# Moving transpositions, key maxima and value sums within the first group of a fused attention and feed-forward kernel

## The chip, the cores and the metric

One Trainium2 chip, one core. The metric is the device time of one execution in microseconds (us), as the median over runs. Engines are named as in the profile: PE (TensorE), DVE (VectorE), ACT (ScalarE), POOL (GpSimd), SP (SyncE, which issues all DMAs here).

## The reference, cut to what matters

Local attention with block summaries for 4 batches, 8 heads, 768 positions and head size 64, then a feed-forward block over 3072 tokens:

```
k_sum = k.reshape(B,H,24,32,D).max(axis=3)      # maximum of each block of 32 keys
v_sum = v.reshape(B,H,24,32,D).mean(axis=3)     # mean of each block of 32 values
scores = concat(scale*q@k.T within a window of 16, scale*q@k_sum.T + log(32))
x = softmax(scores) @ concat(v, v_sum)          # -> (3072, 512)
h = x @ w_in                                    # (3072, 2048)
g = h * tanh(softplus(h));  out = g @ w_out     # (3072, 512)
```

The weights come in as float64 and every product of the feed-forward block is made of three float32r products (high by high, low by high, high by low).

## The kernel before, in words

A **unit** is 256 queries (chunk c of 12, three to a batch) and two heads (hp of 4): 48 units. A **group** of the feed-forward part is 512 tokens, two chunks; there are six groups, and each has 16 **steps**, one for each 128 columns of the hidden layer. The program order of each engine is written out by hand, and every engine works in that order.

The lead-in (L480 to L509, turns u = 0 to 10) makes the eight units of group 0: scores on PE (L321, L323), minus their row maximum on DVE (L339), exponentials on ACT (L343), normalising on DVE and POOL (L353 to L357), transposing on PE with a copy on ACT (L365, L367), values on PE (L397), and the result's high part xh on ACT (L399) and low part xl on DVE (L400). Between these it prepares weights.

A weight **piece** is two steps' worth of w_in or w_out, 1 MB in two DMAs (L124); pieces are numbered w0 to w15 in the order of need (w3 is w_in of steps 4 and 5, w7 of 8 and 9, w11 of 12 and 13). Each passes four calls: *begin* (rebase on ACT L140, two shifts on DVE L144 and L146, after which the next piece is loaded into the freed one of two staging buffers), *join* (DVE L154, L156), *upper* (ACT L164) and *lower* (DVE L171).

The loop L524 runs the steps. Step i issues ff_in(i) on PE (12 products, L412), act(i) and, in the first group, the copy ah(i) on ACT (L419, L428), al(i) on DVE (L430), and at its end ff_out(i-2) on PE (12 products, L440). Into the steps the later units are woven in pairs (n, m). Scores of a pair stand in steps 0, 4, 8, 12, 15, 19 and so on; in the first group the pair is normalised one step later, transposed two steps later (L592, after ff_out), and its values (L397) stand in steps 4, 8, 12 and 15. While pair p stands in its steps, the next pair is prepared: key maxima (km, L250, from the keys' source ks) and value sums (vq, L270 and L271, from vsum), needed only where a new batch begins. In the first group those are the pairs whose scores stand in steps 8 and 12. For such a pair: step 4 (8) takes n's maxima and loads n's vsum (L211); step 5 (9) takes n's sums, stores them (L272) and loads m's ks (L207); step 6 (10) takes m's maxima, loads m's vsum, and POOL copies both units' maxima into the score operands (L281); step 7 (11) takes m's sums, stores them, and loads the next ks if there is one. Step 3 loads the first ks. The sources ks and vsum share a single buffer, so this is one chain of load and reduction. PSUM has four buffers in ps_w for products, scores, transposed blocks and values.

In steps 2, 3, 6, 7, 10 and 11, DVE's order is al(i), then m's maxima or sums, then join, begin and lower. On SP the loads L211, L272 and L207 stand ahead of the piece's load L124 of the same step.

Of the kernel before, what the change touches and what calls it, by code (L numbers as in the profile page):

```python
# [28 lines left out]
CPB = S // CH  # L29
# [3 lines left out]
NFC = DFF // P  # L33
# [19 lines left out]
def _as_f32(bits):  # L53
    import struct
    return struct.unpack("<f", struct.pack("<I", bits))[0]
# [3 lines left out]
def fused_kernel(ctx: ExitStack, tc: tile.TileContext, q0, qk, kt, v0, vw, vs, w_in, w_out, out):  # L59
# [46 lines left out]
    def home(j, part, dtype, name):  # L106

        if j == NW:
            t = stage.tile([P, WB, WP], I64, tag="stage", name=name).bitcast(dtype)
            return t.rearrange("p k f -> p (k f)")[:, :WB * WP]  # L110
        pool = const if j < EARLY else late[0]
        return pool.tile([P, WB * WP], dtype, tag=f"w{part}_{j}", name=name, bufs=1)
# [37 lines left out]
    def join_weight():  # L150
        if begun:
            w, fc, f, x = begun.pop(0)
            u = f.bitcast(U32)
            nc.vector.tensor_scalar(out=f, in0=f, scalar1=-_as_f32(F32_MAX), scalar2=_as_f32(F32_MAX),  # L154
                                    op0=ALU.max, op1=ALU.min)
            nc.vector.scalar_tensor_tensor(out=u, in0=u, scalar=3, in1=x,  # L156
                                           op0=ALU.logical_shift_left, op1=ALU.bitwise_or)
            joined.append((w, fc, f))

    def upper_weight():  # L160
        if joined:
            w, fc, f = joined.pop(0)
            split[w, fc, 0] = home(order[w, fc], 0, F32R, f"w{w}_{fc}_hi")
            nc.scalar.copy(split[w, fc, 0], f)  # L164
            raised.append((w, fc, f))

    def lower_weight():
        if raised:
            w, fc, f = raised.pop(0)
            split[w, fc, 1] = home(order[w, fc], 1, F32R, f"w{w}_{fc}_lo")  # L170
            nc.vector.tensor_sub(split[w, fc, 1], f, split[w, fc, 0].bitcast(F32))  # L171
# [9 lines left out]
    for part, step, at0 in ((blocks[:, :NQ], QT, -WIN), (blocks[:, NQ:], P, CH)):  # L181
        n = part.shape[1]
# [22 lines left out]
    def load_key_source(b, hp):  # L205
        ks = sources[b, hp, 0] = stage.tile([P, S], F32, tag="sum", name=f"ks{b}_{hp}", bufs=1)
        nc.sync.dma_start(ks, kt[b, hp])  # L207

    def load_value_source(b, hp):
        vsum = sources[b, hp, 1] = stage.tile([VP, BLK, BLK], F32, tag="sum", name=f"vsum{b}_{hp}", bufs=1)  # L210
        nc.sync.dma_start(vsum, vs[b, hp].rearrange("p (d j) -> p d j", j=BLK))  # L211
# [11 lines left out]
    def first_key_summary(hp):  # L223
        key_summary(0, hp, keys0[hp][:, WIN:])
# [22 lines left out]
    def key_summary(b, hp, keys):  # L247

        km = att.tile([P, NB], F32, tag="km", name=f"km{b}_{hp}", bufs=HP)
        nc.vector.reduce_max(km, keys.rearrange("p (n j) -> p n j", j=BLK), axis=AX.X)  # L250
        summary[b, hp] = [km]
# [27 lines left out]
    def att_block_keys(c, hp):  # L279
        km = summary[c // CPB, hp][0]  # L280
        nc.gpsimd.tensor_copy(units[c, hp]["qk"][:, :, P + KW:], km.unsqueeze(1).broadcast_to([P, NQ, NB]))  # L281

    def att_summarize_keys(c, hp):
        b, th = divmod(c, CPB)
        if th == 0:
            key_summary(b, hp, sources.pop((b, hp, 0)))
            load_value_source(b, hp)

    def att_summarize_values(c, hp):
        b, th = divmod(c, CPB)  # L290
        if th == 0:
            value_summary(b, hp)
# [66 lines left out]
    def att_transpose(group):  # L359
        pt = att.tile([P, 2 * NQ, P], F32, tag="pt", name=f"pt{group[0][0]}_{group[0][1]}", bufs=1)[:KA]  # L360
        for k, (c, hp) in enumerate(group):
            u = units[c, hp]
            ps = att_psum(c, f"pt_ps{c}_{hp}")
            for s in range(NQ):
                nc.tensor.transpose(ps[:KA, s * P:(s + 1) * P], u["p"][:, s, :], ident)  # L365
            u["pt"] = pt[:, k * NQ:(k + 1) * NQ]
            nc.scalar.copy(u["pt"].rearrange("p s q -> p (s q)"), ps[:KA, :])  # L367
# [54 lines left out]
    def ff_split(g, fc):  # L422

        a = st[g, fc]
        ah = ff.tile([P, TG], F32R, tag="ah", name=f"ah{g}_{fc}")
        al = ff.tile([P, TG], F32R, tag="al", name=f"al{g}_{fc}")

        (nc.scalar.copy if g == 0 else nc.vector.tensor_copy)(ah, a)  # L428
        st[g, fc] = ah, al
        return lambda: nc.vector.tensor_sub(al, a, ah.bitcast(F32))  # L430
# [21 lines left out]
    todo = [(c, hp) for c in range(NCH) for hp in range(HP)]  # L452
    steps = [(g, fc) for g in range(NG) for fc in range(NFC)]

    at = {}
# [7 lines left out]
    n = CG * HP  # L463
# [16 lines left out]
    for u in range(n + 3):  # L480
        if u < n:
            att_scores([todo[u]])
        if 1 <= u <= n:
            att_normalize([todo[u - 1]])
        if 1 <= u <= HP:
            first_value_summary(u - 1)
        lower = att_values([todo[u - 3]]) if 3 <= u else None
        if u in (3, 4):
            window_values(*todo[HP + u - 1])
        if HP < u <= n:  # L490
            block_values(*todo[u - 1])
        if 2 <= u < n + 2:
            att_transpose([todo[u - 2]])
        if u in (0, 2):
            first_key_summary(u + 1)
        if lower:
            lower()
        if u in (3, 9):
            lower_weight()
        if u in (2, 8, 10):  # L500
            join_weight()
            upper_weight()
        if u in (1, 6, 8, 10):
            begin_weight()
            load_weight()
        if u == 1:
            first_key_summary(u + 1)
        if u in (7, 8):
            att_load_values(*todo[u + 1])  # L509
# [5 lines left out]

    turns = sorted(at)
    values = dict(zip(turns[1:] + [turns[-1] + 4], (at[i] for i in turns)))
    turned = {i + 2: group for i, group in at.items() if i < NFC - 1}
    following = dict(zip(turns, (at[i] for i in turns[1:])))
    lower_weight()  # L520
    join_weight()
# [2 lines left out]
    for i in range(len(steps) + 2):  # L524
        if i - 1 in at and i < NFC:
            att_normalize(at[i - 1])
        if i < len(steps):
            ff_in(*steps[i])
            ff_act(*steps[i])
            if i < NFC:  # L530
                split_rest = ff_split(*steps[i])
        if i - 1 in at:
            upper_weight()
            rebase_weight()
        if i < NFC and i - 1 in following:

            att_summarize_values(*following[i - 1][0])
        group = values.get(i)
        lower = att_values(group) if group else None
        if lower and i >= NFC:  # L540
            lower()
        if i in at:
            att_scores(at[i], i >= NFC - 1)
        if i < NFC:
            if lower:
                lower()
            split_rest()
        if i - 1 in at and i >= NFC:
            att_normalize(at[i - 1])
        if i - 3 in at and i - 3 >= NFC - 1:  # L550
            att_transpose_blocks(at[i - 3], 1)
        if NFC <= i < len(steps):
            ff_split(*steps[i])()
        if i - 2 in at and i - 2 >= NFC - 1:
            att_transpose_blocks(at[i - 2], 0)
        if i - 3 in following:
            n, m = following[i - 3]
            att_summarize_values(*m)
            after = todo.index(m) + 1
            if after < len(todo) and todo[after][0] % CPB == 0:  # L560
                load_key_source(todo[after][0] // CPB, todo[after][1])
        if i in following:
            n, m = following[i]
            att_summarize_keys(*n)
            for unit in (n, m):
                att_load_keys(*unit)
        if i - 1 in following:
            n, m = following[i - 1]
            if i >= NFC:
                att_summarize_values(*n)  # L570
            if m[0] % CPB == 0:
                load_key_source(m[0] // CPB, m[1])
        if i - 2 in following:
            n, m = following[i - 2]
            att_summarize_keys(*m)
            for unit in (n, m):
                att_block_keys(*unit)
        if i not in at:
            upper_weight()
        join_weight()  # L580
        begin_weight(i in at)
        load_weight()
        if i not in at:
            lower_weight()
        if i - 1 in at:
            lower_weight()
        if group:
            for unit in at.get(i, ()):
                att_load_values(*unit)
        if i >= 2:  # L590
            ff_out(*steps[i - 2])
        if i in turned:  # L592
            att_transpose(turned[i])


# [42 lines left out]
```

## Time and profile before

| | us |
|---|---|
| median of 3 runs (633.32 to 637.02) | 635.2 |
| the profiled execution's own time | 637.01 |
| its span | 635.1 |
| PE busy in it | 606.7 |
| DVE busy | 384.4 |
| ACT busy | 258.9 |

The span is the stretch from the first to the last instruction; times in rows count from its start. Busy is the union of an engine's instructions. In a row of the timeline, the bracket at the end gives how long the engine sat idle just before and which instruction's end released it.

### The profile page before, as it was taken

What the parts mean: (1) busy time and instruction counts of PE and PEld (TensorE: products, weight loads), DVE (VectorE), ACT (ScalarE), POOL (GpSimd) and SP (SyncE); (2) the same over time, 40 slices, a digit from 0 to 9 for tenths busy, and PEclk for the clock granted to TensorE, in tenths of its full rate; (3) what the DMA queues carried; (4) which work ended last, traced back from release to release, by engine and by line L of the source; (5) the groups of instructions that cost most, each with busy time, mean ns of one, the idle gap of its engine ahead of it and who ended that gap; (6) DMA issues with size and microseconds to landing.
All of it is one profiled execution on the core that took longest, in us unless ns stands there. A gap on an engine that the chain in (4) does not pass through costs nothing.

```text
span 635.1 us, 10801 instructions
## 1 busy us (share of the span) xinstructions
PE 606.7 (96%) x4096; PEld 496.5 (78%) x4096; DVE 384.4 (61%) x1032; ACT 258.9 (41%) x630; POOL 75.9 (12%) x119
## 2 busy tenths in 40 slices
PE   4858998899999999999999999999999999999997
PEld 3746876778888888788888888888888888888886
DVE  4678998884656668756637659757547546222211
ACT  3768875768144144253153253253352241111111
POOL 3441010102011010120110110110110110000000
PEclk9979999999999999999999999999999999999999
DMA  8946686733123042632032242532231110100001
GB/s 274 325 148 244 224 271 206 262 123 97 67 96 102 20 146 63 206 117 92 4 96 88 82 144 72 171 98 69 87 103 59 38 33 0 67 0 1 0 1 66
DMA packets 31779, 69.26 MB, mean 109 GB/s; under 512 B 4720, under 2 KB 11120, under 8 KB 31728
## 3 DMA queue, kind: packets, MB, share of 16 engines
q1 hardware_dynamic: 31728, 68.58, 33.8%
q8 instruction: 32, 0.52, 0.3%
q14 instruction: 19, 0.16, 0.1%
HBM read 60.16 MB, written 6.29 MB: 105 GB/s over the span
## 4 chain that ended last, share of the span: by engine, by line
PE 78%; DVE 8%; ACT 5%; DMA 4%; issue 3%; SPq 1%; POOL 0%; DVEq 0%; ACTq 0%; POOLq 0%
PE po L440 36%; PE ph L412 34%; PE x_ps L397 3%; PE sc L317 2%; DMA ks<-kt 2%; ACT pr L343 2%; DVE w_lo L171 2%; DMA vw<-vw 1%; DVE x L144 1%; DVE f L154 1%; ACT f L140 1%; DVE x L146 1%; DMA w<-w_out 1%; DVE km L250 1%; DVE al L430 1%
## 5 line engine op out<-in xcount | busy, mean ns | idle before, releaser
L419 ACT ACTIVATE a<-ph 128x512 f32<-128x512 f32 x96 | 57.4, 598 | 283.7 <-PE ph L412 230.2
L412 PE MATMUL ph<-xh,w_hi 128*128 128x512 f32 x384 | 151.2, 394 | 2.5 <-DVE nm L339 2.3
L440 PE MATMUL po<-w_hi,ah 128*128 128x512 f32 x384 | 152.0, 396 | 0.2 <-DVE o L448 0.2
L412 PE MATMUL ph<-xl,w_hi 128*128 128x512 f32 x384 | 150.3, 391 | 0.0
L412 PE MATMUL ph<-xh,w_lo 128*128 128x512 f32 x384 | 150.2, 391 | 0.0
L440 PE MATMUL po<-w_lo,ah 128*128 128x512 f32 x384 | 149.7, 390 | 0.0
L440 PE MATMUL po<-w_hi,al 128*128 128x512 f32 x384 | 149.6, 390 | 0.0
L428 DVE CAST ah<-a 128x512 fp32r<-128x512 f32 x80 | 34.8, 435 | 143.9 <-ACT a L419 143.4
L378 DVE STREAM_TRANSPOSE pt<-pr 32x256 f32<-32x256 f32 x256 | 111.6, 436 | 3.6
L412 PEld LDWEIGHTS ph<-xh,w_hi 128*128 128x128 f32 x384 | 72.6, 189 | 18.8 <-issue 2.1
L440 PEld LDWEIGHTS po<-w_hi,ah 128*128 128x128 f32 x384 | 72.1, 188 | 18.0 <-issue 3.0
L412 PEld LDWEIGHTS ph<-xh,w_lo 128*128 128x128 f32 x384 | 72.5, 189 | 15.3
L412 PEld LDWEIGHTS ph<-xl,w_hi 128*128 128x128 f32 x384 | 72.6, 189 | 14.8
L440 PEld LDWEIGHTS po<-w_lo,ah 128*128 128x128 f32 x384 | 72.1, 188 | 15.3
L440 PEld LDWEIGHTS po<-w_hi,al 128*128 128x128 f32 x384 | 72.2, 188 | 14.3
L343 ACT ACTIVATE pr<-pr,nm 128x120 f32<-128x120 f32 x192 | 73.2, 382 | 19.3 <-DVE nm L339 19.0
L357 POOL TENSOR_TENSOR pr<-pr,rs 128x960 f32<-128x960 f32 (+1 forms) x28 | 44.3, 1581 | 225.3 <-DVE rs L354 147.2
L430 DVE TENSOR_TENSOR al<-a,ah 128x512 fp32r<-128x512 f32 x96 | 66.6, 694 | 6.5 <-ACT ah L428 3.8
L397 PEld LDWEIGHTS x_ps<-pt,vw 120*64 120x64 f32 x768 | 26.0, 143 | 16.7 <-issue 8.6
L400 DVE TENSOR_TENSOR xl<-x_ps,xh 128x512 fp32r<-128x512 f32 (+1 forms) x28 | 17.2, 613 | 34.9 <-ACT xh L399 34.5
L397 PE MATMUL x_ps<-pt,vw 120*64 120x64 f32 x768 | 29.8, 231 | 8.2 <-POOL pr L357 3.7
L343 ACT ACTIVATION_READ_ACCUMULATOR pr<-pr,nm 128x1 f32 x192 | 35.8, 187 | 0.0
(59 smaller groups left out, 455.8 us busy)
## 6 DMA issues: line engine op xcount, KB each, us to landing
qk<-qk SPq DMA_DIRECT2D x40, 496.0 KB, 4.2
vw<-vw SPq DMA_DIRECT2D x48, 192.0 KB, 5.2
w<-w_in SPq DMA_DIRECT2D x16, 512.0 KB, 4.6
w<-w_out SPq DMA_DIRECT2D x16, 512.0 KB, 4.6
ks<-kt SPq DMA_DIRECT2D x16, 384.0 KB, 4.4
out<-o SPq DMA_DIRECT2D x24, 256.0 KB, 2.3
vsum<-vs SPq DMA_DIRECT2D x12, 384.0 KB, 3.3
vw<-vm SPq DMA_DIRECT2D x40, 48.0 KB
```

What stands on the lines that cost most here:

```text
L171: nc.vector.tensor_sub(split[w, fc, 1], f, split[w, fc, 0].bitcast(F32))
L317: nc.tensor.matmul(ps[h][row, at0:at0 + KA], u["qk"][r, s, h * QT:(h + 1) * QT], u["qk"][r, s, P:], start=True, stop=True)
L343: nc.scalar.activation(pr[:, j, :], pr[:, j, :], AF.Exp, scale=-1.0, bias=nm[:, j:j + 1], accum_out=sm[:, j:j + 1])
L357: nc.gpsimd.tensor_mul(u["pr"], u["pr"], rs.unsqueeze(2).broadcast_to([P, n, KA]))
L378: nc.vector.transpose(u["tr"][b * SQ:(b + 1) * SQ, :, a * SQ:(a + 1) * SQ], u["wide"][a * SQ:(a + 1) * SQ, :, b * SQ:(b + 1) * SQ])
L397: nc.tensor.matmul(x, u["v"][:, s, d], pt, start=True, stop=True)
L400: return lambda: nc.vector.tensor_sub(xl, x, xh.bitcast(F32))
L412: nc.tensor.matmul(ph, w[:, cc * P:(cc + 1) * P], x[:, cc, :], start=(cc == 0 and n == 0), stop=(cc == NCC - 1 and n == 2))
L419: nc.scalar.activation(a, st[g, fc], AF.Mish)
L428: (nc.scalar.copy if g == 0 else nc.vector.tensor_copy)(ah, a)
L430: return lambda: nc.vector.tensor_sub(al, a, ah.bitcast(F32))
L440: nc.tensor.matmul(po[g][t], a[:, tok], w, start=(fc == 0 and n == 0), stop=(fc == NFC - 1 and n == 2))
```

## The change

In the lead-in, w1 begins in turn 7 and not 6, its *upper* comes in turn 9 and not 8 (so after w2's *begin*), and its *lower* in turn 10 and not 9. In the first group the transposition of a pair moves from the end of the second step after its scores (behind ff_out) into the third (behind ff_in, act and ah). The calls for m's maxima and the copies (step 2, 6, 10, 14) and for m's sums with the next ks (step 3, 7, 11, 15) move, in the first group alone, from ahead of the step's weight work to behind it. From step 16 on, the order is what it was.

```
-        if u in (3, 9):
+        if u in (3, 10):
             lower_weight()
         if u in (2, 8, 10):
             join_weight()
+        if u in (2, 9, 10):
             upper_weight()
-        if u in (1, 6, 8, 10):
+        if u in (1, 7, 8, 10):
             begin_weight()
             load_weight()
...
-    turned = {i + 2: group for i, group in at.items() if i < NFC - 1}
+    turned = {i + 3: group for i, group in at.items() if i < NFC - 1}
...
             if i < NFC:
                 split_rest = ff_split(*steps[i])
+            if i in turned:
+                att_transpose(turned[i])
...
-        if i - 3 in following:
-            n, m = following[i - 3]
-            att_summarize_values(*m)
-            ...
-                load_key_source(todo[after][0] // CPB, todo[after][1])
+        def last_sum():
+            if i - 3 in following:
+                ... the same five lines
+        def last_maxima():
+            if i - 2 in following:
+                n, m = following[i - 2]
+                att_summarize_keys(*m)
+                for unit in (n, m):
+                    att_block_keys(*unit)
+        if i >= NFC:
+            last_sum()
...
-        if i - 2 in following:
-            ...
+        if i >= NFC:
+            last_maxima()
         if i not in at:
             upper_weight()
         join_weight()
         begin_weight(i in at)
         load_weight()
         ...
             lower_weight()
+        if i < NFC:
+            last_maxima()
+            last_sum()
         ...
             ff_out(*steps[i - 2])
-        if i in turned:
-            att_transpose(turned[i])
```

## Rows read from the trace of the kernel before

**Rows 1.** The page's line of busy time by engine.

```profile
PE 606.7 (96%) x4096; PEld 496.5 (78%) x4096; DVE 384.4 (61%) x1032; ACT 258.9 (41%) x630; POOL 75.9 (12%) x119
```

**Rows 2.** Busy time by stretch: the stretch, its length, then the busy us of each engine (instructions), PE's granted clock, DMA share, GB/s.

```profile
100.00:125.00 25.00, 20.98 (x106) 16.49 (x107) 24.33 (x47) 16.77 (x32) 3.30 (x3) 1.00 0.75 238
...
150.00:300.00 150.00, 149.80 (x1027) 122.95 (x1024) 98.42 (x292) 58.66 (x155) 17.46 (x24) 1.00 0.33 104
```

**Rows 3.** PE's timeline, the rows with an idle time of note before them, and the values of step 15: start, us, engine, line, operation, operands.

```profile
38.78 0.42 PE L397 MATMUL x_ps<-pt,vw 120*64 120x64 f32 x7 [2.88 <-POOL pr L357]
...
62.54 0.65 PE L365 MATMUL pt_ps<-ident,pr 128*120 128x128 f32 x4 [1.83 <-POOL pr L357]
...
88.82 0.43 PE L365 MATMUL pt_ps<-ident,pr 128*120 128x128 f32 x2 [1.10 <-POOL pr L357]
...
100.20 0.64 PE L317 MATMUL sc<-qk 64*64 64x120 f32 x16 [0.45 <-POOL qk L281]
...
111.27 0.47 PE L412 MATMUL ph<-xh,w_hi 128*128 128x512 f32 x1 [1.53 <-DVE nm L339]
...
119.09 0.65 PE L365 MATMUL pt_ps<-ident,pr 128*120 128x128 f32 x4 [2.12 <-POOL pr L357]
...
140.07 0.47 PE L412 MATMUL ph<-xh,w_hi 128*128 128x512 f32 x1 [0.79 <-DVE nm L339]
...
149.35 1.15 PE L397 MATMUL x_ps<-pt,vw 120*64 120x64 f32 x32
```

**Rows 4.** DVE's timeline in the lead-in: xl of the last four units, each behind an idle time, and the first L339 of step 0.

```profile
38.23 0.42 DVE L400 TENSOR_TENSOR xl<-x_ps,xh 128x256 fp32r<-128x256 f32 x1 [1.04 <-ACT xh L399]
...
39.91 0.42 DVE L400 TENSOR_TENSOR xl<-x_ps,xh 128x256 fp32r<-128x256 f32 x1 [0.65 <-ACT xh L399]
...
44.92 0.42 DVE L400 TENSOR_TENSOR xl<-x_ps,xh 128x256 fp32r<-128x256 f32 x1 [0.95 <-ACT xh L399]
...
47.04 0.42 DVE L400 TENSOR_TENSOR xl<-x_ps,xh 128x256 fp32r<-128x256 f32 x1 [0.56 <-ACT xh L399]
...
54.78 0.28 DVE L339 CUSTOM_DVE_ANT_0 pr<-sc,base 128x120 f32<-128x120 f32 x1
```

**Rows 5.** DVE's timeline in steps 4 to 10: the first L339 of step 4 and of step 8, the four key maxima L250, the low parts al ahead of two of them, and the *lower* that ends step 6's weight work.

```profile
79.56 0.27 DVE L339 CUSTOM_DVE_ANT_0 pr<-sc,base 128x120 f32<-128x120 f32 x1
...
82.38 0.94 DVE L250 TENSOR_REDUCE km<-ks 128x24 f32<-128x768 f32 x1
...
94.92 0.68 DVE L430 TENSOR_TENSOR al<-a,ah 128x512 fp32r<-128x512 f32 x1
98.47 0.95 DVE L250 TENSOR_REDUCE km<-ks 128x24 f32<-128x768 f32 x1 [2.87 <-DMA ks<-kt]
...
102.49 1.21 DVE L171 TENSOR_TENSOR w_lo<-f,w_hi 128x1024 fp32r<-128x1024 f32 x1
...
109.84 0.27 DVE L339 CUSTOM_DVE_ANT_0 pr<-sc,first 128x120 f32<-128x120 f32 x1
...
112.66 0.94 DVE L250 TENSOR_REDUCE km<-ks 128x24 f32<-128x768 f32 x1
...
125.19 0.69 DVE L430 TENSOR_TENSOR al<-a,ah 128x512 fp32r<-128x512 f32 x1
128.52 0.95 DVE L250 TENSOR_REDUCE km<-ks 128x24 f32<-128x768 f32 x1 [2.64 <-DMA ks<-kt]
```

**Rows 6.** SP's timeline: the issue of the first ks, of w10 (step 3), and of the sums' store in step 7.

```profile
74.59 0.42 SPq L207 DMA_DIRECT2D ks<-kt  x1
78.61 0.92 SPq L124 DMA_DIRECT2D w<-w_out  x2
...
105.68 0.80 SPq L272 DMA_DIRECT2D vm<-vq  x1
```

**Rows 7.** DMA issues by kind: count, KB each, median us from issue to landing.

```profile
w<-w_out SPq DMA_DIRECT2D x16, 512.0 KB, 4.6
ks<-kt SPq DMA_DIRECT2D x16, 384.0 KB, 4.4
...
vsum<-vs SPq DMA_DIRECT2D x12, 384.0 KB, 3.3
```

**Rows 8.** The chain that ended last, in order of time: start, us, what.

```profile
123.14 5.36 DMA ks<-kt
...
145.79 0.87 PE pt_ps L365 x8
...
154.43 2.72 PE ph L412 x12
```

**Rows 9.** POOL's timeline: the copy of m's maxima that the scores of step 8 wait for.

```profile
99.64 0.51 POOL L281 COPY qk<-km 128x96 f32<-128x96 f32 x1 [9.52 <-DVE km L250]
```

**Rows 10.** Groups of instructions by line and shape: busy us, mean ns of one, idle before.

```profile
L419 ACT ACTIVATE a<-ph 128x512 f32<-128x512 f32 x96 | 57.4, 598 | 283.7 <-PE ph L412 230.2 <-issue 53.3
...
L428 ACT CAST ah<-a 128x512 fp32r<-128x512 f32 x16 | 10.0, 622 | 0.5
L367 ACT COPY pt<-pt_ps 120x512 f32<-120x512 f32 x16 | 8.9, 586 | 0.4 <-PE pt_ps L365 0.4
```

**Rows 11.** Busy time by stretch, around two idle times of PE; columns as in Rows 2, PE's granted clock third from the end.

```profile
41.00:50.00 9.00, 6.51 (x44) 5.23 (x44) 7.46 (x10) 3.84 (x6) 2.31 (x3) 0.50 0.43 151
118.00:120.00 2.00, 0.91 (x9) 0.91 (x9) 1.97 (x4) 2.00 (x3) 2.00 (x2) 1.00 0.94 269
```

More of the change, by code (lines that the diff above doesn't have):

```diff
@@ L555, in fused_kernel @@
             att_transpose_blocks(at[i - 2], 0)
-        if i - 3 in following:
-            n, m = following[i - 3]
-            att_summarize_values(*m)
-            after = todo.index(m) + 1
-            if after < len(todo) and todo[after][0] % CPB == 0:
-                load_key_source(todo[after][0] // CPB, todo[after][1])
+        def last_sum():
+            if i - 3 in following:
+                n, m = following[i - 3]
+                att_summarize_values(*m)
+                after = todo.index(m) + 1
+                if after < len(todo) and todo[after][0] % CPB == 0:
+                    load_key_source(todo[after][0] // CPB, todo[after][1])
+        def last_maxima():
[6 more added lines that the diff above has]
+            last_sum()
         if i in following:
@@ L572, in fused_kernel @@
                 load_key_source(m[0] // CPB, m[1])
-        if i - 2 in following:
[L574 to L577, printed above, removed]
+        if i >= NFC:
+            last_maxima()
         if i not in at:
```

## The prediction

> **What bounds the kernel now.** I began with the page's busy line: PE is busy for 606.7 of 635.1 us [rows 1], so only some 28 us can be gained on it at all. Busy time by stretch says where: from 150 us on PE has no idle time worth naming (149.80 of 150 up to 300 us), while between 100 and 125 us it is busy for 20.98 of 25 and DVE for 24.33 [rows 2]. So the lead-in and the first group decide, and a change there counts by one thing: how much earlier PE comes to its gapless run, which begins with ff_in(14) at 140.07. PE's timeline shows what it waits for: POOL's normalised scores ahead of three transpositions (1.83, 1.10, 2.12), POOL's copy of m's maxima (0.45), and DVE's L339 of steps 8 and 12, which must free a PSUM tile (1.53, 0.79) [rows 3]. DVE's timeline shows why DVE is late: in steps 6 and 10 it stands idle for 2.87 and 2.64 us until the keys' source has landed, with weight work behind [rows 5].
>
> **The lead-in.** DVE's work from 38 us to the first L339 at 54.78 stays the same; what can go is its four waits for xh, 1.04 + 0.65 + 0.95 + 0.56 = 3.2 us [rows 4]. w1's shifts no longer stand ahead of the seventh unit's L339, and w1's *upper* no longer holds ACT, waiting for the join, ahead of w2's rebase and xh. The first wait remains, since xl still follows xh of its unit and w1's shifts now stand behind it: 1.0. The later ones find xh done while DVE joins and shifts. Gain for DVE: 2.2 us; bounds 0 (waits that only move) and 3.2. In steps 0 and 1 ACT, which waits for the same joins, comes as much earlier, so I carry about 2.3 to step 4: its L339 at 77.3 for 79.56 [rows 5].
>
> **The first ks.** L207 of step 3 now stands on SP behind w10's two DMAs, which are issued once w8's shifts are done: 78.61 - 2.3 = 76.3, plus 0.92 to issue them, so ks goes out at 77.2 for 74.59 [rows 6]. Its landing is bounded by 3.3 us (vsum, the same size) and 5.36 (the slow ks) [rows 7, 8]; I take 4.7, a little over the 4.4 of its kind, because 1 MB stands just ahead. So 81.9, bounds 80.5 and 82.6. DVE is ready 2.82 after L339 (79.56 to 82.38 [rows 5]), at 80.1. **It waits some 1.8 us, and L250 stands at 81.9 for 82.38: of the 2.3 gained, 0.5 is left.** Behind the wait stand join and begin of step 4, the normalising and n's sums. The Trainium skill ("DMA: Bandwidth & Descriptors", Queues, rings and completion order) says that each DMA engine takes the descriptors of a queue in ring order; by that ks lands behind the weights, and if it overtook them, at the 3.3 bound, the sum below would be 1.4 better. No row before shows the two in this order.
>
> **Steps 4 to 8.** The 2.87 us wait in step 6 goes: join, begin and lower stand there now, and ks has landed when they end. L339 of step 8: 109.84 - 0.5 - 2.87 = 106.5, and PE's 1.53 goes. But m's maxima come later in the order. al(6) ends at 95.60 - 0.5 = 95.1; the weight work is 103.70 - 99.42 = 4.3; L250 runs from 99.4 to 100.35 for 98.47 to 99.42 [rows 5]. POOL's copy and PE follow by 0.22 + 0.51 + 0.05 [rows 3, 9]: the second half of step 8's scores starts at 101.1 for 100.20, **0.9 later**. PE stands there for some 2 us in place of 0.45. Between that point and ff_in(10) lie 111.27 - 1.53 - 100.20 = 9.5 us [rows 3]; ff_in(10) starts at 110.6 for 111.27. The PSUM tile is free by 107.9 (before, the wait ended 1.43 after its L339), so it holds nothing up any more. m's vsum goes out at 100.4, behind w13's load on SP, and even at 4.6 lands by 105.0; m's sums stand at 100.35 + al 0.65 + weights 4.3 = 105.3, so they need not wait. m's ks, landed at 98.47 before, would do at 99.4 even if it came no earlier.
>
> **The transpositions.** Each now follows an ff_in (2.72 us [rows 8]). POOL's three waits, 5.05 us together, are covered by it; the cover of the first two is worth nothing by itself, since PE runs into the waits for w_lo, for the copies of pt and for the scores just told. Its price is in step 15, where the transposition and the values of the same pair now stand in one step: PE transposes for 0.87 [rows 8], but ACT first does act, 0.60, ah, 0.62, and the first copy, 0.59 [rows 10]. PE stands 1.81 - 0.87 = **0.95 us**; bounds 0 (something later holds PE anyway) and 1.5 (both copies).
>
> **The third ks** (of step 7). Its load follows m's sums, which are now DVE's last work ahead of L339: sums end at 106.5, the store takes 0.80 [rows 6], L207 goes at 107.4. By then w14 has landed, so I take the 3.3 of vsum: 110.7, bounds 110.7 and 112.8 (5.36). DVE is ready at 106.5 + 2.8 = 109.3 and waits 1.4; L250 at 110.7 for 112.66. From there to the end of al(10) it is 125.88 - 112.66 = 13.2 [rows 5], so 123.9; weight work 4.3, L250 to 129.2, copy and PE 0.8: **the second half of step 12's scores starts at 130.0**. Before, it started when the 128.52 maxima were done, at 129.47 + 0.8 = 130.25 by the same steps. Gain 0.25. PE arrives at about 127 (110.6 + five blocks of 2.72 + 0.87 + values and half of the scores, some 1.7) and stands 3 us.
>
> **The sum.** From there PE is gapless but for 0.79, which goes (L339 of step 12 comes earlier by 2.64 and more), and the 0.95 that comes. -0.25 - 0.79 + 0.95 = -0.1 us. On the profiled execution, 637.0 us of its own time for a span of 635.1: 636.9. It lies 1.8 above the median 635.2; so I forecast **635.1 for the median**. The bounds: ks of step 3 shifts everything by -1.4 to +0.7, that of step 7 by 0 to +2.1, step 15 by -0.95 to +0.55: as a sum rarely all at once, 633.0 to 637.8. A measurement of this kernel tells some 0.5% (3.2 us) from no change.
>
> **Rivals.**
> A, the waits at the transpositions count in full: PE is what is late, not the chain of ks and DVE. For it: they are real waits of PE, 5.05 us. Against: DVE's 24.33 of 25, and L250 behind the weight work. 635.2 - 5.05 = 630.1. Chance 0.13.
> B, PE's clock falls in the new wait of 3 us in step 12. In the lead-in an idle time of 2.88 us [rows 3] came ahead of a stretch of 9 us at clock 0.50, the 1.2 GHz level; after the 2.12 in step 10 the clock stayed at 1.00 [rows 11]. The wait I expect is nearer to the first, which did other, light work around it. It decides where PE's idle time comes to about 2.9. Price: half of PE's busy 6.51 up to half of 9, 3.3 to 4.5 us; with -0.1 and the larger, 639.5, which is slower. Chance 0.14. The Trainium skill ("TensorE: Matmul & The Clock Gate", HAM oscillation) says that TensorE left without work falls to half clock and must earn the full one again; it speaks against a change that gathers short waits into a long one.
> C, DVE gains nothing in the lead-in. ks of step 3 then lands at 84.2, and all behind it comes 2.3 later: 637.4, still no change. Chance 0.15.
> Forecast 0.58.
>
> **How the numbers follow.** Faster by over 0.5% is A, 0.13, with a little of the forecast's lower edge: 0.15. Slower is most of B, 0.12, and the worst landings of both ks, 0.02: 0.14. The rest, 0.71, is within 0.5%. The range holds the forecast, C, the smaller halves of A and B (half of 5.05 is 632.7; 3.3 is 638.4): 631.7 to 638.5.
>
> **What would show it.** Right: PE's row for the scores of step 8 and of step 12 idle for 2 to 3 us behind POOL L281; DVE idle ahead of L250 in steps 4 and 8, not in 6 and 10; no PE wait at L365; 0.9 us idle at L397 in step 15; PE gapless from there within 1 us of the old place (values of step 15 at 149.35 before [rows 3]). Wrong: L250 of steps 4 and 8 without a wait; L281 done ahead of PE; a clock below 1.00 after step 12; or step 0's L339 still near 54.8.

## The result, and the profile after

The changed kernel takes 638.7 us (median of 10 runs, 636.8 to 641.1); the kernel before, measured beside it, 635.9 (10 runs, 633.3 to 639.2). The ratio is 1.0052, 95% interval 1.0034 to 1.0070: **slower by 2.9 us**, where no change was forecast. The profiled execution of the changed kernel took 641.06 us (span 639.3), that of the kernel before 637.01.

Busy time by stretch, columns as in [rows 2]:

```profile
100.00:125.00 25.00, 21.73 (x107) 17.86 (x108) 23.29 (x45) 17.42 (x34) 3.66 (x3) 0.93 0.77 248
150.00:300.00 150.00, 148.85 (x1039) 122.17 (x1037) 95.15 (x274) 57.24 (x147) 17.42 (x25) 1.00 0.30 97
```

Past 150 us PE is as busy as before but for one wait (0.95, below). In every profile of this study the run's own time, less the start of step 15's values, is 487.6 to 487.9 us (637.01 - 149.35 = 487.66 before, 641.06 - 153.20 = 487.86 after). So the place of that one row tells the time of an execution: 149.35 before [rows 3], 153.20 after.

DVE after, answering to [rows 4, 5]:

```profile
36.71 0.42 DVE L400 TENSOR_TENSOR xl<-x_ps,xh 128x256 fp32r<-128x256 f32 x1 [1.04 <-ACT xh L399]
...
52.84 0.27 DVE L339 CUSTOM_DVE_ANT_0 pr<-sc,base 128x120 f32<-128x120 f32 x1
...
63.48 0.69 DVE L154 TENSOR_SCALAR f<-f 128x1024 f32<-128x1024 f32 x1 [1.24 <-ACT f L140]
...
78.84 0.27 DVE L339 CUSTOM_DVE_ANT_0 pr<-sc,base 128x120 f32<-128x120 f32 x1
...
84.14 0.95 DVE L250 TENSOR_REDUCE km<-ks 128x24 f32<-128x768 f32 x1 [2.40 <-DMA ks<-kt]
...
101.55 0.94 DVE L250 TENSOR_REDUCE km<-ks 128x24 f32<-128x768 f32 x1
...
108.70 0.28 DVE L339 CUSTOM_DVE_ANT_0 pr<-sc,first 128x120 f32<-128x120 f32 x1
...
112.83 0.95 DVE L250 TENSOR_REDUCE km<-ks 128x24 f32<-128x768 f32 x1 [1.22 <-DMA ks<-kt]
...
125.37 0.69 DVE L430 TENSOR_TENSOR al<-a,ah 128x512 fp32r<-128x512 f32 x1
125.97 0.69 DVE L154 TENSOR_SCALAR f<-f 128x1024 f32<-128x1024 f32 x1
...
130.25 0.97 DVE L250 TENSOR_REDUCE km<-ks 128x24 f32<-128x768 f32 x1
```

One of the four waits for xh is left, and L339 of step 0 comes 1.94 us earlier, as worked out. The waits ahead of L250 have changed sides: none in steps 6 and 10, 2.40 and 1.22 in steps 4 and 8. In step 10 the weight work (five operations) now stands between al (125.37) and the maxima (130.25).

ACT's row behind DVE's wait at 63.48, and SP's for w10 and the first ks [rows 6]:

```profile
50.76 1.14 ACT L140 ACTIVATE f<-w 128x1024 f32<-128x1024 f32 x1 [1.23 <-DMA w<-w_out]
```

```profile
77.90 0.80 SPq L124 DMA_DIRECT2D w<-w_out  x2
78.74 0.43 SPq L207 DMA_DIRECT2D ks<-kt  x1
```

PE, answering to [rows 3], and POOL's two copies [rows 9]:

```profile
103.27 1.08 PE L317 MATMUL sc<-qk 64*64 64x120 f32 x16 [3.53 <-POOL qk L281]
...
113.52 0.39 PE L412 MATMUL ph<-xh,w_hi 128*128 128x512 f32 x1
...
132.60 0.64 PE L317 MATMUL sc<-qk 64*64 64x120 f32 x16 [2.75 <-POOL qk L281]
...
153.20 1.17 PE L397 MATMUL x_ps<-pt,vw 120*64 120x64 f32 x32 [0.95 <-ACT pt L367]
```

```profile
102.71 0.51 POOL L281 COPY qk<-km 128x96 f32<-128x96 f32 x1 [10.82 <-DVE km L250]
...
131.44 1.11 POOL L281 COPY qk<-km 128x96 f32<-128x96 f32 x1 [10.87 <-DVE km L250]
```

No transposition and no ff_in waits any more, the ff_in at 113.52 included. PE's idle time has been gathered into two waits for m's maxima, and there are new ones for the copies of pt: 0.95 in step 15, and 1.78 ahead of the values of step 4 (72.60). Behind both score waits the granted clock (third from the end) falls to 0.50, the 1.2 GHz level:

```profile
102.00:104.00 2.00, 0.73 (x16) 0.70 (x16) 1.97 (x4) 1.95 (x4) 0.51 (x1) 0.72 0.87 330
104.00:106.00 2.00, 2.00 (x12) 1.43 (x5) 2.00 (x3) 0.50 (x1) 0.00 (x0) 0.50 1.02 336
...
132.00:134.00 2.00, 1.40 (x19) 1.10 (x20) 1.97 (x3) 0.00 (x0) 0.55 (x1) 0.90 0.67 197
134.00:136.00 2.00, 2.00 (x7) 1.52 (x6) 1.97 (x3) 0.00 (x0) 0.00 (x0) 0.50 0.00 0
136.00:138.00 2.00, 2.00 (x8) 1.64 (x7) 2.00 (x18) 1.58 (x9) 0.00 (x0) 0.75 0.04 6
```

Between step 12's second half of scores and step 15's values lie 20.60 us; before there were 19.10, 0.79 of waiting among them.

Two theories were set against each other. **K**: the loss is the late start of m's maxima, behind the weights. **Q**: it is the granted clock behind PE's gathered wait. The rival to both was that the loss lies in another part of the change.

### The profile page after: what moved, and what is told of

Its sections match the earlier page's. It is cut to its first block, busy times and chain, and to the rows that moved or that the text cites. A ratio compares the mean times of both kernels' runs of the same rounds, so it can differ in the third digit from the quotient of the medians.

```text
span 639.3 us, 10797 instructions
## 1 busy us (share of the span) xinstructions
PE 608.0 (95%) x4096; PEld 497.4 (78%) x4096; DVE 384.3 (60%) x1032; ACT 259.2 (41%) x630; POOL 75.5 (12%) x119
## 4 chain that ended last, share of the span: by engine, by line
PE 78%; DVE 8%; DMA 7%; ACT 3%; issue 3%; SPq 0%; POOL 0%; DVEq 0%; POOLq 0%; ACTq 0%
PE po L440 37%; PE ph L412 34%; PE x_ps L397 3%; PE sc L317 3%; DMA ks<-kt 2%; DMA w<-w_out 2%; DMA q<-qk 1%; DVE x L144 1%; DMA vw<-vw 1%; DVE w_lo L171 1%; ACT pr L343 1%; DMA vsum<-vs 1%; DVE x L146 1%; DVE f L154 1%; DVE km L250 1%
## 5 line engine op out<-in xcount | busy, mean ns | idle before, releaser
L339 DVE CUSTOM_DVE_ANT_0 pr<-sc,base 128x120 f32<-128x120 f32 x128 | 31.4, 276 | 8.2 <-PE sc L317 7.6
```

Of the source, the lines that this page charges most:

```text
L339: nc.vector.tensor_tensor_reduce(out=pr[:, j, :], in0=ps[h][:, at0:at0 + KA], in1=m, scale=-SCALE, scalar=-NEG, op0=ALU.add, op1=ALU.min, ...
```

## The experiments: one part of the change alone

Four kernels, each the kernel before with one part of the diff and nothing else, on one chip (before: 635.26 us).

The lead-in's three conditions alone:

```
-        if u in (3, 9):
+        if u in (3, 10):
             lower_weight()
         if u in (2, 8, 10):
             join_weight()
+        if u in (2, 9, 10):
             upper_weight()
-        if u in (1, 6, 8, 10):
+        if u in (1, 7, 8, 10):
             begin_weight()
             load_weight()
```

> The kernel before with the lead-in's edits alone. Theory K (the end of the first group is set by when POOL has copied m's maxima ahead of the scores of steps 8 and 12, and the change puts those copies later): the lead-in alone moves no maxima, so DVE's first L339 comes about 1.9 us earlier (54.78 to 52.9), some 0.7 of it is left at step 4, and the end moves by 0 to -0.7 us. Theory Q (the loss is mostly PE's clock, which falls in waits made longer): PE gets a wait of over 4 us for act(0) ahead of ff_in(2), the clock falls there, and if that reached the end it would cost 1.5 to 2.5 us; I expect it to be hidden behind DVE. Ratio 0.999 to 1.000 by K, up to 1.004 if the clock's fall counts.

634.73 us, ratio 0.9994 [0.9973, 1.0015]. Its profile, of a run at the median (634.65), has L339 of step 4 at 77.31, just where the prediction had it, and DVE's waits in steps 6 and 10 are still 2.67 and 2.25 us.

The transpositions alone:

```
-    turned = {i + 2: group for i, group in at.items() if i < NFC - 1}
+    turned = {i + 3: group for i, group in at.items() if i < NFC - 1}
...
                 split_rest = ff_split(*steps[i])
+            if i in turned:
+                att_transpose(turned[i])
...
             ff_out(*steps[i - 2])
-        if i in turned:
-            att_transpose(turned[i])
```

> The kernel before with the transpositions in the third step alone. K: maxima and sums stay, so the scores of steps 8 and 12 start where they did (100.2 and 130.25); the covered waits for POOL (1.83, 1.10, 2.12 us) only become longer waits at the scores, and step 15 costs 0.95 us for the copies: +0.9 us. Q: PE now stands about 3 us at the scores of steps 8 and 12, the clock falls there and some 1.5 us more is lost after step 12: +2 to +2.5 us. A third view, that the transpositions' waits counted in full: -5 us.

636.11 us, 1.0017 [0.9994, 1.0040]. In its profile the waits at L365 are gone and step 15 has its wait of 0.95; nothing is gained in the median. (The profiled run, 633.97, is 2.1 below it.)

The maxima and copies alone (`last_maxima` holds the lines that stood there):

```
+        if i >= NFC:
+            last_maxima()
         if i not in at:
             upper_weight()
...
         if i - 1 in at:
             lower_weight()
+        if not (i >= NFC):
+            last_maxima()
```

> The kernel before with m's maxima and the copies behind the weight work alone (sums where they were). K: the copies come 1.4 us later (maxima at about 99.9 instead of 98.47), so the second half of the scores of steps 8 and 12 starts about 1.4 us later, and m's sums now wait for vsum on DVE, about 3 us, ahead of the weight work: +0.6 to +1.4 us. Q: the waits at the scores grow to about 2 us only, the clock stays up and the cost is no more than K's. If the late maxima cost nothing, the theory K is wrong.

639.13 us, 1.0063 [1.0040, 1.0086]: slower by itself. With m's sums left where they were, DVE also runs into this:

```profile
106.70 1.22 DVE L270 TENSOR_REDUCE vq<-vsum 96x32 f32<-96x1024 f32 x1 [6.70 <-DMA vsum<-vs]
```

m's vsum goes out only behind the late maxima, at 99.43, behind a weight load, and lands 7.25 us later. The change avoids this by moving the sums last as well, so this kernel does not price the move within the change.

The sums and the next ks load alone (`last_sum` likewise):

```
+        if i >= NFC:
+            last_sum()
         if i in following:
...
         if i - 1 in at:
             lower_weight()
+        if not (i >= NFC):
+            last_sum()
```

> The kernel before with m's sums and the next source's load behind the weight work alone. K: the first ks is issued behind w10's two DMAs, lands at about 84.5 instead of 79, and L250 of step 4 stands at 84.5 for 82.38; the ks of step 8 is issued at about 110.7 for 106.6 and L250 there at about 114 for 112.66; the scores of step 12 start 1 to 2 us later: +1 to +2 us. Q: as K, plus a fall of the clock if PE's wait in step 12 passes 2.7 us. If the load's place behind the weights does not matter: 0.

637.35 us, 1.0030 [1.0009, 1.0050]: slower too. DVE waits 2.59 and 1.05 us ahead of L250 in steps 4 and 8, as in the changed kernel. PE needs no wait at the scores of step 12 here; it stands 3.24 us for POOL's normalised scores at the transposition of step 10 (120.19), with a clock of 0.60 and 0.55 behind it. So this part alone does not lose its time by way of m's maxima.

## The experiments: one part undone

Each is the changed kernel with one thing put back (before on that chip: 636.32 us).

The first ks load ahead of the weight load in step 3:

```
-        if i >= NFC:
+        if i >= NFC or i == 3:
             last_sum()
...
             last_maxima()
-            last_sum()
+            if i != 3:
+                last_sum()
```

> The changed kernel with the first ks load of step 3 put back ahead of that step's weight load. K: DVE's wait of 2.4 us ahead of L250 in step 4 goes, everything up to step 12's scores comes about 2 us earlier, and so does the end: 2 us less than the changed kernel, ratio to before about 1.002. Q (clock): the waits at the scores stay as long, the clock still falls, the gain is the same 2 us or less. If the place of that load does not matter, nothing is gained (1.005).

638.27 us, but from 633.7 to 643.1; 1.0024 [0.9997, 1.0051]. The profiled run was the fastest of its runs and has L250 of step 4 at 78.63 without a wait, L339 of step 4 already at 75.81. Inconclusive in the median.

The maxima and copies ahead of the weights again:

```
-        if i >= NFC:
-            last_maxima()
+        last_maxima()
...
         if i < NFC:
-            last_maxima()
             last_sum()
```

> The changed kernel with m's maxima and the copies put back ahead of the weight work, the rest kept. K: the copies for the scores of steps 8 and 12 come some 3.4 us earlier than in the changed kernel, PE's waits there (3.53 and 2.75 us) go or shrink under 1 us, the clock stays up, and DVE's L339 of steps 8 and 12 set the place of ff_in(10) and ff_in(14) again: 2.5 to 3.5 us less than the changed kernel, ratio about 1.000. If the loss sits in the sums or in step 15 instead: ratio 1.003 to 1.005.

635.50 us, 0.9991 [0.9978, 1.0004]: **this one move undone takes back the whole loss**. Its profile shows no wait in the scores of steps 8 and 12 and a granted clock of 1.00 from 48 us on, though L250 of step 4 comes as late as 85.01; the waits of L250 in steps 6 and 10 have shrunk to 0.17 and 0.22 us. It does not tell K from Q, since both go with the wait.

The last pair transposed in step 14, as before:

```
-    turned = {i + 3: group for i, group in at.items() if i < NFC - 1}
+    turned = {i + 3: group for i, group in at.items() if i < NFC - 4}
...
             ff_out(*steps[i - 2])
+        if i == NFC - 2:
+            att_transpose(at[i - 2])
```

> The changed kernel with the last pair of the group transposed at the end of step 14, as before, and the other three in the third step. All theories: PE's wait of 0.95 us ahead of the values of step 15 goes, as nothing later holds PE: 0.9 to 1.0 us less than the changed kernel, ratio about 1.0035. If the wait was hidden by something later: 1.005.

638.95 us, 1.0051 [1.0034, 1.0068]. Step 15's wait of 0.95 is gone in the profile; the median does not show so little.

The first unit's scores of steps 8 and 12 computed five times, to keep PE at work in its waits:

```
+        again = 5 if group[0] in ((3, 0), (3, 2)) else 1
-        for k, unit in enumerate(group):
+        for k, unit in [(0, group[0])] * (again - 1) + list(enumerate(group)):
```

> The changed kernel in which the scores of the first unit of steps 8 and 12 are computed five times instead of once, so that PE works for some 2 us more in each of its two waits; results are the same. Q: the clock stays at 1.00 after both waits, and the 1.6 us lost after step 12 (with up to 0.9 after step 8) comes back: 1.5 to 2.5 us less than the changed kernel, ratio 1.001 to 1.003. K alone, with no cost of the clock: no difference (1.005), or slower by what the repeated scores last beyond the wait, which is nothing here.

639.49 us, 1.0052 [1.0031, 1.0073]. The clock stays at 1.00 behind both waits in the profile, and 19.01 us lie from step 12's scores to step 15's values for 20.60. No gain in the median: against Q, or a gain too small for these runs.

## The experiments: which place, and the clock

Next the two places were taken apart (before on that chip: 635.73 us). Maxima ahead in step 10 alone, for the pair of step 12:

```
-        if i >= NFC:
+        if i >= NFC or i == 10:
             last_maxima()
...
         if i < NFC:
-            last_maxima()
+            if i != 10:
+                last_maxima()
```

> The changed kernel with the last unit's maxima and copies ahead of the weights again in step 10 alone (for the pair of step 12); in step 6 they stay last. Theory K (the place of the maxima costs the time, and the last such place before PE's gapless run decides): the second half of step 12's scores needs no wait, starts near 129.9 for 132.60, and the wait of 3.5 us in step 8 stays; the whole of the loss comes back: values of step 15 at 150.4, or at 148.8 if the clock too stays at full, time 2.8 to 4.4 us below the changed kernel's profiled 641.1; median about 635.7. Rival (each place costs its own share): half of the loss, median about 637.3.

635.86 us, 1.0004 [0.9988, 1.0021]. Step 12's scores start at 127.13 without a wait, though step 8's still wait 3.21:

```profile
100.97 0.64 PE L317 MATMUL sc<-qk 64*64 64x120 f32 x16 [3.21 <-POOL qk L281]
...
127.13 1.05 PE L317 MATMUL sc<-qk 64*64 64x120 f32 x32
...
147.07 1.17 PE L397 MATMUL x_ps<-pt,vw 120*64 120x64 f32 x32 [0.95 <-ACT pt L367]
```

Maxima ahead in step 6 alone, for the pair of step 8 (the same diff with 6 for 10):

> The changed kernel with the last unit's maxima and copies ahead of the weights again in step 6 alone (for the pair of step 8); in step 10 they stay last. Theory K: the wait in step 8's scores goes (they start near 100), but the chain through DVE, the third ks (issued behind the same sums, landed near 112.8) and the maxima of step 10 stays where it is; PE comes earlier to step 12's scores and waits there for 5 us and more instead of 2.8; no gain, median about 638.7. Rival (each place costs its own share): half of the loss, median about 637.3.

640.33 us, 1.0071 [1.0050, 1.0092]: nothing comes back. PE arrives earlier at step 12's scores and waits there, 3.54 us rather than the 5 expected, since it has first waited 1.61 for L339. **The loss hangs on step 10's move**, as K had it, and the rival of equal shares fell.

The lead-in put back as before, all else as changed (the first diff of the four parts, reversed):

> The changed kernel with the lead-in's three conditions as before; transpositions, maxima and sums as changed. By the prediction the lead-in's edits carry 2.3 us to step 4, of which the first ks (queued behind w10, which comes as much later) gives back nothing here: 2.3 us longer than the changed kernel, 641.0. By what the changed kernel's profile shows (ACT waits for w4, and only 0.7 us is carried): 0.7 us longer, 639.4. First ks lands 0.7 to 2.3 later than 84.1.

640.28 us, 1.0075 [1.0054, 1.0095], about 1.5 us slower than the changed kernel (by the two ratios, whose intervals overlap). L339 of step 4 stands at 80.73, L250 at 86.21 and step 12's scores at 134.63: within the change the lead-in is most likely a gain, of 1.5 us or a little more, between the prediction's 2.3 and the 0.7 that the one profile after showed.

The clock was still open. Two pairs were run on one chip (before: 636.17 us), in each of which one kernel repeats the first unit's scores, as above but in step 12 alone:

```
+        again = 6 if group[0] == (3, 2) else 1     # 5 in the second pair
```

First pair, on the kernel with the maxima ahead in step 6, with the repeats and without:

> The changed kernel with the maxima ahead in step 6 alone, and the first unit's scores of step 12 computed six times, which fills some 2.2 of the 3.5 us that PE waited there. Theory Q (the granted clock's fall after that wait is part of the loss): clock 1.00 after step 12's scores, 19.0 us from them to step 15's values for 21.6, median 1.5 to 2.5 us below x2. Rival (the chain alone): no difference in the median.

> The changed kernel with the maxima ahead in step 6 alone, once more: the companion of x1 on the same chip. Median about 640, PE's wait in step 12's scores 3.5 us and a granted clock of 0.50 behind it.

638.39 us, 1.0041 [1.0022, 1.0060], with the repeats, 641.11 us, 1.0077 [1.0051, 1.0103], without; the means of 9 and 8 runs differ by 2.3 +- 1.5 us. PE's rows of both, and the granted clock behind step 12's scores (the repeats shift lines by one):

```profile
130.68 0.64 PE L318 MATMUL sc<-qk 64*64 64x120 f32 x16 [1.46 <-POOL qk L281]
149.69 1.17 PE L398 MATMUL x_ps<-pt,vw 120*64 120x64 f32 x32 [0.95 <-ACT pt L368]
```

```profile
132.00:134.00 2.00, 2.00 (x10) 1.64 (x10) 2.00 (x3) 0.00 (x0) 0.00 (x0) 1.00 0.15 47
134.00:136.00 2.00, 2.00 (x11) 1.65 (x10) 1.97 (x13) 0.83 (x5) 0.00 (x0) 1.00 0.00 0
```

```profile
131.49 1.08 PE L317 MATMUL sc<-qk 64*64 64x120 f32 x16 [3.72 <-POOL qk L281]
153.07 1.17 PE L397 MATMUL x_ps<-pt,vw 120*64 120x64 f32 x32 [0.95 <-ACT pt L367]
```

```profile
132.00:134.00 2.00, 2.00 (x16) 1.41 (x9) 2.00 (x3) 0.00 (x0) 0.00 (x0) 0.50 0.25 92
134.00:136.00 2.00, 2.00 (x6) 1.60 (x5) 1.97 (x11) 0.69 (x4) 0.00 (x0) 0.50 0.00 0
```

19.01 us against 21.58 for the same work: the clock costs 2.6 us here, and a PE that does useless work is quicker, clear of the noise though not by much. Q holds for this kernel.

Second pair, the changed kernel with repeats and unaltered:

> The changed kernel with the first unit's scores of step 12 computed five times (step 8 left as it is), which fills some 1.8 of the 2.75 us that PE waited there. Theory Q: clock 1.00 behind step 12's scores, median about 1.5 us below x4. Rival (the chain alone): no difference in the median.

> The changed kernel once more, unaltered: the companion of x3 on the same chip. Median about 638.7, ratio about 1.005.

638.31 us, 1.0034 [1.0018, 1.0049], and 638.57 us, 1.0039 [1.0022, 1.0055]; means of 12 runs each differ by 0.3 +- 1.0 us. Here Q fails in the median. The unaltered kernel's new profile (638.59 us, at its median) shows that the clock need not fall in step 12:

```profile
131.68 0.64 PE L317 MATMUL sc<-qk 64*64 64x120 f32 x16 [1.37 <-POOL qk L281]
150.73 1.17 PE L397 MATMUL x_ps<-pt,vw 120*64 120x64 f32 x32 [0.95 <-ACT pt L367]
```

```profile
104.00:108.00 4.00, 4.00 (x18) 3.07 (x11) 4.00 (x5) 1.06 (x1) 0.00 (x0) 0.57 0.72 187
132.00:134.00 2.00, 2.00 (x23) 1.52 (x13) 1.97 (x3) 0.00 (x0) 0.00 (x0) 1.00 0.57 180
134.00:136.00 2.00, 2.00 (x10) 1.67 (x9) 1.97 (x4) 0.00 (x0) 0.00 (x0) 1.00 0.00 0
```

The first of these rows lies behind a wait of 3.17 in step 8, and there the clock fell, as in the first profile. PE came to step 12 only some 0.5 us later than in that one (129.67 for 129.20); what made its wait so much shorter, 1.37 for 2.75, is mostly that it was released 0.92 earlier: m's maxima stand at 129.96 for 130.25, and POOL's copy took 0.51 for 1.11 us:

```profile
131.12 0.51 POOL L281 COPY qk<-km 128x96 f32<-128x96 f32 x1 [10.83 <-DVE km L250]
```

The wait of step 12 ends when DVE's chain has come through, whatever PE has waited before; that is why step 6's move undone gives nothing: PE then meets step 12 early, and waits there for long. The 1.5 us of clock in the first profile (a run 2.3 us above its median) are therefore not paid in every execution.

Last, a kernel made of what the runs spoke for: the changed one with the maxima ahead again, the first ks load ahead of the weight load, and the last pair transposed in step 14 (that part of the edit as in u3 above, left out here):

```
-        if i >= NFC:
+        if i >= NFC or i == 3:
             last_sum()
...
-        if i >= NFC:
-            last_maxima()
+        last_maxima()
...
-        if i < NFC:
-            last_maxima()
+        if i < NFC and i != 3:
             last_sum()
```

> The changed kernel with three things undone: maxima and copies ahead of the weights in steps 6 and 10, the first ks load of step 3 ahead of the weight load, and the last pair of the first part transposed in step 14 as before. What is left of the change: the lead-in, the first three pairs transposed in the third step, the unit's sums last in steps 7 and 11 (and in step 3 before the weights). By theory K: no wait at DVE's L250 of steps 4, 6 and 10, none of PE at the scores of steps 8 and 12, none at step 15's values; against the kernel with the maxima ahead alone (635.5, 0.9991) the 0.95 us of step 15 goes, and up to 2 us where the first ks held DVE: median 632.5 to 634.5, ratio 0.995 to 0.998. Rival (something else bounds PE at that point, the DVE work of steps 4 to 12): 635, ratio 0.999.

634.17 us, **0.9964 [0.9945, 0.9983]**, the only version whose interval lies below 1, by 2.3 us (1.6 between the medians). DVE still waits for ks in three steps, so the rows that were expected without a wait have one; PE's scores need none:

```profile
79.54 0.94 DVE L250 TENSOR_REDUCE km<-ks 128x24 f32<-128x768 f32 x1
...
96.14 0.95 DVE L250 TENSOR_REDUCE km<-ks 128x24 f32<-128x768 f32 x1 [3.38 <-DMA ks<-kt]
...
111.54 0.95 DVE L250 TENSOR_REDUCE km<-ks 128x24 f32<-128x768 f32 x1 [1.10 <-DMA ks<-kt]
...
125.79 0.95 DVE L250 TENSOR_REDUCE km<-ks 128x24 f32<-128x768 f32 x1 [1.01 <-DMA ks<-kt]
```

## Why the prediction was wrong

It forecast 635.1; the changed kernel takes 638.7, 3.6 more. The order of events was right at nearly every point; sizes were not. The table sets the prediction's steps against the profiles in which each could be read (the changed kernel's and those of experiments that leave that step as changed):

| step | predicted | mean (profiles) | lowest to highest |
|---|---|---|---|
| L339 of step 4 | 77.3 | 77.4 (13) | 75.81 to 79.46 |
| first ks, issue to landing | 4.7 | 5.5 (10) | 5.07 to 5.71 |
| L250 of step 4 | 81.9 | 83.1 (10) | 81.85 to 85.01 |
| second half of step 12's scores | 130.0 | 131.5 (8) | 130.28 to 132.60 |
| from there to step 15's values | 19.25 | 19.0 (4), PE's wait up to 1.46 | 20.6 (2), 2.59 and 2.75; 21.6 (2), over 3.5 |

The last line's 20.6 stands for the changed kernel's first profile and u3, with the 0.95 added that u3 avoids in step 15.

**The lead-in** was right, near enough: step 0 as worked out, and 77.4 in step 4 against a mean of 79.4 in the five profiles with the old lead-in (78.21 to 80.73), a gain of 1.9 for 2.3. (The four waits less the first give 2.2; the prediction carried 2.3.) The first profile's 78.84 holds a DMA wait of ACT, 1.23, that x4 (0.96) and u2 (0.87) have too and p1, u1 and w10 have not; judged by that one profile, the lead-in would have been called the failing step, which p1 contradicts.

**The first ks: the first step that failed.** It does wait behind w10, but 5.5 us, not 4.7; seven of the ten landings lie above the upper bound, 5.36, and none below 5.07. That bound was not the slowest ks of the trace it was taken from. The chain that ended last in the kernel before [rows 8] also holds this one, issued in step 5:

```profile
92.50 5.95 DMA ks<-kt
```

No cover is left behind it: the 1.2 late at L250 comes out as 1.5 at step 12's scores. The Trainium skill ("DMA: Bandwidth & Descriptors", Queues, rings and completion order) says that each DMA engine takes a queue's descriptors in ring order; the runs agree with it so far as ks right behind the weights landed after 5.07 us or more each time, and the third ks, sent 3.25 us behind its weights, after 3.17 (first profile).

**Steps 6 and 10: the second, and the dearer one.** The prediction took it that the waits of 2.87 and 2.64 of the profile of before [rows 5] would go and pay for the 4.3 us of weight work put there; with what the earlier steps give, it found PE's scores 0.9 later in step 8 and 0.25 earlier in step 12. From L250 of step 4 on its steps do come out: 48.1 us from there to step 12's scores, 47.9 in x4 and 48.5 in the first profile. What it did not see is that the old order would have lost these waits anyway, because the change makes ks late in steps 4 and 8.

In the profiles that keep the old order they are 2.87, 2.67, 0.45, 0.98, 0.17, 0.67, 3.38, 0.64 and none in step 6 (before, p1, p2, p4, u2, w6, v1, x1, x2), and 2.64, 2.25, 1.01, 0.60, 0.22, 0.72 and 1.01 in step 10 (before, p1, p2, p4, u2, w10, v1). Where DVE has already waited for ks two steps earlier (in step 4: p4, u2, w6, x1, x2; in step 8: p4, u2, w10, v1), the wait is 1.01 at most; where it has not, it is 2.25 or more, but for p2. By these rows the old order takes up a late ks in these waits, and the new one does the 4.3 of weights first all the same. In u2, which is the changed kernel with the old order here, L250 of steps 4, 6 and 10 stands so:

```profile
85.01 0.95 DVE L250 TENSOR_REDUCE km<-ks 128x24 f32<-128x768 f32 x1 [2.65 <-DMA ks<-kt]
...
98.41 0.95 DVE L250 TENSOR_REDUCE km<-ks 128x24 f32<-128x768 f32 x1 [0.17 <-DMA ks<-kt]
...
127.32 0.95 DVE L250 TENSOR_REDUCE km<-ks 128x24 f32<-128x768 f32 x1 [0.22 <-DMA ks<-kt]
```

From L250 of step 4 to that of step 10 it is 42.3 us in u2 and 43.4 in w10, 46.1 and 46.2 in the changed kernel (first profile, x4): some 3 us, which is the loss, and u2 and w10 take it back.

**The sum's last step** failed with it: 1.8 us were taken off because the profile of before lay that far above its median (1.2 above the median of ten). In x4, a run at the changed kernel's median, step 15's values stand at 150.73, 1.5 behind the 149.25 that the sum amounts to. That is the chain's share of the 3.6; most of the rest is this offset, which did not carry over. Why not stays open. That the profile of before was slow because its waits in steps 6 and 10 were long is one reading; p2 speaks for it (a quick run with short ones) and p1 against it (a run at its median with waits of 2.67 and 2.25).

**The gapless stretch** was taken at full clock. That is right for x4 and wrong for the first profile and u3's, where rival B came in part: in the first, the wait of 2.75 was followed by 0.50, but cost 1.5, not 3.3 to 4.5, because the clock was back at 138. The Trainium skill ("TensorE: Matmul & The Clock Gate", HAM oscillation) says that TensorE left without work falls to half clock; in step 12 the rows show that fall behind waits of 2.59 us and more, and none behind 1.81 and less. The length of the wait alone does not tell it, though: elsewhere the clock fell behind 2.10 (p1) and stayed behind 2.71 (v1).

**Right as written**: no wait at L365; waits at L250 of steps 4 and 8 only; the PSUM tile no longer held; 0.95 us in step 15, to the hundredth (its own terms give 0.94); the third ks, landed in 3.17 us for 3.3; the places of PE's two score waits, though not their sizes: forecast as 2 and 3 us, they are 3.53 and 2.75 in the first profile and 3.17 and 1.37 in the second. **Rival A** fell: without the waits at the transpositions (p2) nothing is gained. **Rival C** fell with the lead-in's 1.9 us.

## What to carry to other kernels

A wait for a load is also slack: it takes up what comes late ahead of it. Before trading it for fixed work, ask what else in the same change comes late and would have gone into it, and how short it is in other executions, because the fixed work is paid in all of them. When a load is put behind a larger one on its queue, take the landing at the slow end and follow it to the next gapless run; take that slow end from every row of its kind, not from one. Gathering short waits into one long one can also cost clock, so leave the consumer's last dependence (here m's maxima) ahead of work that nobody waits for yet.

## What was not expected of the hardware

- ks, 384 KB right behind 1 MB of weights on one queue, landed in 5.07 to 5.71 us in ten profiles; the third one, sent 3.25 us behind its weights, in 3.17 in the profile after. But the one of 5.95 in the kernel before went out 4.9 us behind the last weights, and the same load, sent the same way, took 4.0 in p2, so the place behind the weights is not all that counts. A vsum of 384 KB, sent 1.9 us behind a weight load, took 7.25 (p3).
- With one lead-in, L339 of step 4 varied by 3.7 us between executions, more than the effect under study.
- Behind waits of 2.48 us (u1, step 8) and 2.59 to 3.72 (step 12) the granted clock fell to 0.50 to 0.60; behind 2.12 [rows 3, 11] and 1.81 it did not. Yet in p1 it fell behind a wait of 2.10 at the same transposition as the 2.12, and in v1 it stayed at 1.00 behind 2.71 in step 4:

```profile
116.64 1.09 PE L365 MATMUL pt_ps<-ident,pr 128*120 128x128 f32 x8 [2.10 <-POOL pr L357]
118.00:120.00 2.00, 2.00 (x6) 1.59 (x5) 2.00 (x3) 1.41 (x2) 0.00 (x0) 0.51 0.98 358
```

```profile
71.07 1.17 PE L397 MATMUL x_ps<-pt,vw 120*64 120x64 f32 x32 [2.71 <-ACT pt L367]
72.00:74.00 2.00, 2.00 (x46) 1.64 (x41) 1.97 (x3) 2.00 (x3) 0.00 (x0) 1.00 0.88 281
```

- Repeating 2 us of useless scores in the wait of step 12 kept the clock at 1.00 and made the first pair's kernel 2.3 +- 1.5 us quicker.
- The same POOL copy of m's maxima, L281, took 0.51 us, and in six of the profiles one of its two took 1.11, with PE's scores waiting for it.
